# A Fourier filter with an FFN behind it: the first transform of seven batches in three products of rounded parts

## The chip, the cores and the metric

The kernel runs on one core of a Trainium2 chip. Five engines work side by side, each through its own queue in order: TensorE (PE) multiplies matrices into PSUM, VectorE (DVE), ScalarE (ACT) and GpSimd (POOL) work elementwise, and SyncE (SP) issues the transfers. The metric is device time in microseconds of one launch; lower is better.

## The reference

A batch of 8 sequences of 3008 tokens with 256 channels goes through a real Fourier transform along the sequence, a complex 256 x 256 product, a soft threshold and the inverse transform. The result goes through a gated FFN.

```python
X = np.fft.rfft(x, axis=1)
Yr = Xr @ w_r - Xi @ w_i + b_r
Yi = Xr @ w_i + Xi @ w_r + b_i
Yr = np.sign(Yr) * np.maximum(np.abs(Yr) - lam, 0.0)
Yi = np.sign(Yi) * np.maximum(np.abs(Yi) - lam, 0.0)
y = np.fft.irfft(Y, n=x.shape[1], axis=1)
...
g = x @ w_gate
silu = g * (1.0 / (1.0 + np.exp(-g)))
val = x @ w_val
return (silu * val @ w_out).astype(np.float32)
```

## The kernel before

The length 3008 is 47 x 64, and the transform is done as two small transforms in a row. `stage_a` (L290) does the one of length 47: a chunk of x, 96 x 512, is multiplied by the constant `wa` (96 x 96) in one fp32 product (L295), ScalarE copies the result out of PSUM (L298), and it goes to device memory as d1 (L299). There are 16 chunks to a batch, 128 in all. `stage_b` (L304) reads a pair of rows of d1 and does the transform of length 64 (L311); ScalarE copies it out (L315), GpSimd adds real and imaginary parts (L316), and DVE makes two rounded parts of it, `f_hi` (L318) and `f_lo` (L319).

A number in two parts, hi (rounded to the fp32r type) and lo (what the rounding left, also fp32r), is multiplied in three products, hi by hi, lo by hi and hi by lo, as the table `PASSES` says. `stage_mix` (L322) does the complex product so (L329, L337), with a bias added on DVE (L331) between its two halves. Then comes the soft threshold: ScalarE copies t out of PSUM (L349), DVE clamps it to y (L350), GpSimd subtracts (L351), ScalarE rounds to `y_hi` (L354), DVE takes `y_lo` (L355). `stage_bi` (L357) is the first inverse transform, again in three products (L365, L368), copied out by ScalarE (L370) and stored as d2. `stage_ai` (L384) does the second one in fp32 (L388), with a copy out for each half of the channels (L395). Meanwhile `load_seven` (L236) unpacks and splits the FFN's weights on DVE (L223 to L232), GpSimd (L233 to L247, L255) and ScalarE (L254), 18 times.

The order of this part is written as a table of slots. A slot is one pair of rows p of one batch b: stage_b at slot s, stage_mix at s + 1, stage_bi at s + 2, with 12 slots to a batch and 8 batches. The chunks of batches 1 to 7 are put beside them: the first 40 at 2.7 to a slot, the other 72 spread evenly up to slot 84. A chunk is loaded at slot s and goes through stage_a at s + 1. The chunks of batch 0 run before the slots begin. Weight steps begin at slot 14, one block each 4.3 slots. This is the order in which the code is written; the framework's scheduler then gives each engine its own queue order by a timeline of its own. An engine starts its instructions in that order, and one that waits holds all behind it.

The chunks land in five places of 512 columns in a tile named `scratch`. The pools that matter are `early`, `late`, `k1p` and `z`; the class `sb` says by a tag which pool a tile is from.

Behind the transform, `gated_ffn` multiplies the result by the FFN's weights (L516 is the line of all its products), in an order written by hand.

Of the kernel before, what the change touches and what calls it, by code (L numbers as in the profile page):

```python
# [10 lines left out]
F32R = mybir.dt.float32r  # L11
I32 = mybir.dt.int32
AF = mybir.ActivationFunctionType
ALU = mybir.AluOpType
# [3 lines left out]
P = 128  # L18
B = 8
# [8 lines left out]
NCH = NM // CM  # L28
# [4 lines left out]
T = 512  # L33
# [8 lines left out]
LEAD = 1  # L42
X_FAST, X_RATE, X_END = 40, 2.7, 84
# [70 lines left out]
def f32(ap):  # L114
    return ap.bitcast(F32)


PASSES = ((0, 0), (0, 1), (1, 0))


@with_exitstack
def spectral_ffn(ctx: ExitStack, tc: tile.TileContext, xp, w_r, w_i, cb, wup_raw, wdn_raw, ca, cf, ci, co, out):
    nc = tc.nc
    const = ctx.enter_context(tc.tile_pool(name="const", bufs=1))
    dram = ctx.enter_context(tc.tile_pool(name="dram", bufs=2, space=DRAM))
    wdn = [const.tile([P, NQ, 7, P], F32R, name=f"wdn_{p}") for p in ("hi", "lo")]
    ring = ctx.enter_context(tc.tile_pool(name="ring", bufs=RING, reuse_waits="tile"))
    xt_d = [dram.tile([P, 2, SEQ], F32, name=f"xt_d{b}", bufs=1) for b in range(B)]
    d2 = {B - 1: dram.tile([NK, P, C], F32, name="d2_last", bufs=1)}
    wup_d = [dram.tile([P, 2, 7 * P], F32, name=f"wup_d{u}", bufs=1) for u in range(2 * NQ)]  # L130


    front = ctx.enter_context(tc.tile_pool(name="front", bufs=1))
    ps_ = ctx.enter_context(tc.tile_pool(name="ps", bufs=1, space=PSUM))

    with ExitStack() as tail:
        last = tail.enter_context(tc.tile_pool(name="last", bufs=2, side="right"))
        with ExitStack() as one:
            finish = transform(one, tc, front, last, ps_, xp, w_r, w_i, cb, wup_raw, wdn_raw, ca, cf, ci, co, wdn, wup_d, xt_d, d2)
        finish()  # L140
        ffn = gated_ffn(ctx, tc, front, ring, ps_, co, wdn, wup_d, xt_d, d2[B - 1], out)
        next(ffn)
    next(ffn, None)


def transform(ctx, tc, front, last, ps_, xp, w_r, w_i, cb, wup_raw, wdn_raw, ca, cf, ci, co, wdn, wup_d, xt_d, d2):
    nc = tc.nc
    v = nc.vector

    pools = [ctx.enter_context(tc.tile_pool(name=n, bufs=b)) for n, b in (("early", 2), ("late", 2), ("k1p", 1), ("z", 2))]  # L150
    k1p = pools[2]

    class sb:
        at = dict(a_in=0, a=0, f=0, f_hi=0, f_lo=0, raw=1, t=1, y=1, y_hi=1, y_lo=1, both=1, z=3)

        def tile(shape, dtype, name, tag, **kw):
            return pools[sb.at[tag]].tile(shape, dtype, name=name, tag=tag, **kw)
# [9 lines left out]


    wa = k1p.tile([96, 96], F32, name="wa")
    wi = [k1p.tile([P, 2, P], F32R, name=f"wi_{p}") for p in ("hi", "lo")]  # L170
    wmix = [[k1p.tile([P, 2, C], F32R, name=f"wm{i}_{p}") for p in ("hi", "lo")] for i in range(3)]
    bias = []
# [2 lines left out]

    def load_wa():
        nc.sync.dma_start(wa, ca)

    def load_wf(i):
        sl = slice(i, i + 6)  # L180
        nc.sync.dma_start(wf[:, sl, :], cf[:, sl, :])
# [82 lines left out]
    def paced(fn):  # L264
        with tc.issue_after(gates[-1].ins) if gates else ExitStack():
            return fn()

    def load_x(b, ch):
        t = take()
        nc.sync.dma_start(t, xp[b, ch])  # L270
        return t
# [3 lines left out]
    def load_first():  # L275
# [11 lines left out]
            res += [t[:, i * T : (i + 1) * T] for i in range(n)]  # L287
        return res

    def stage_a(b, ch, xt):  # L290
        if ch == 0:
            d1[b] = dram.tile([NK, P, C], F32, name="d1", tag="d1")
        tag = "absz"[ch % 4] if b == 0 else "a"
        ps = ps_.tile([P, T], F32, name="ps_a", tag="ps_" + tag)
        nc.tensor.matmul(ps[:96], lhsT=wa, rhs=xt, start=True, stop=True)  # L295
        tag = "azt"[ch % 3] if b == 0 else "a"
        a = sb.tile([96, T], F32, name="a", tag=tag)
        nc.scalar.copy(a, ps[:96])  # L298
        store = nc.sync.dma_start(d1[b].rearrange("k (q m) c -> (k q) (m c)", m=NM)[:, ch * T : (ch + 1) * T], a)  # L299
        if b == 0 and ch == NCH - 1:  # L300
            gates.append(store)
# [100 lines left out]
    def at(slot, fn):  # L402
        slots.setdefault(int(slot), []).append(fn)

    xs, zs, fs, ys, box = {}, {}, {}, {}, {}
# [5 lines left out]
    for b in range(B):  # L411
        base = NP * b
        for p in range(NP):
            s = base + p
# [2 lines left out]
            at(s + 2, lambda b=b, p=p: stage_bi(b, p, ys.pop((b, p))))  # L417
    for k in range((B - 1) * NCH):
        b, ch = k // NCH + 1, k % NCH
        s = k / X_RATE if k < X_FAST else X_FAST / X_RATE + (k - X_FAST) * (X_END - LEAD - X_FAST / X_RATE) / ((B - 1) * NCH - X_FAST)  # L420
        at(s, lambda b=b, ch=ch: xs.__setitem__((b, ch), paced(lambda: load_x(b, ch))))
        at(s + LEAD, lambda b=b, ch=ch: stage_a(b, ch, xs.pop((b, ch))))
    for k in range((B - 1) * NU):
        b, u = divmod(k, NU)
        s = NP + Z_FIRST + k / Z_RATE if k < Z_LATE else Z_AT + (k - Z_LATE) * Z_STEP
# [11 lines left out]
    for _ in range(WARM):  # L437
        nc.tensor.matmul(mixed[0][:, :C], lhsT=warm[:, :P], rhs=warm[:, C:], start=True, stop=True)
    load_wa()
    first = load_first()  # L440
    gates.append(first_load[-1])
    paced(lambda: load_wf(0))
    for ch in range(NCH):
        stage_a(0, ch, first[ch])
# [374 lines left out]
```

## Time and profile before

| | us |
|---|---|
| median of 3 runs | 2769.14 |
| lowest and highest | 2768.75, 2771.31 |
| the profiled execution's own time | 2764.52 |
| its span in the profile | 2762.6 |
| last product of the inverse transform, start | 674.20 |
| first product of the FFN, start | 676.61 |

In the profile, a group of instructions is a line of the code, an engine and an operation, with the tiles it writes and reads; "busy" is the time in which at least one of them ran, the mean is that of one instruction, and "idle before" is how long the engine stood still ahead of them, and for whom. A wait is written as who waited, for whom, how long in total, how often, and the longest. An fp32 product is recorded as two matmuls, an fp32r product as one.

### The profile page before, as it was taken

How to read it: one execution, taken by the hardware profiler on the slowest of the kernel's cores; microseconds unless marked ns; L12 is line 12 of the kernel's file. 1: busy time of each engine (PE TensorE's matmuls, PEld its weight loads, DVE VectorE, ACT ScalarE, POOL GpSimd, SP SyncE). 2: the span in 40 equal slices, each digit the busy share in tenths (PEclk: the TensorE clock that was granted, in tenths of full speed). 3: DMA queues.
4: the chain of work that ended last, by engine and by line, in shares of the span. 5: the costliest groups of instructions: out<-in, count | busy, mean ns of one | idle time of the engine just before them, and what ended most of it. 6: DMA issues, size and time to landing. Idle time of an engine off the chain costs nothing. (4 is left out here: it accounts for less than half of the span.)

```text
span 2762.6 us, 39633 instructions
## 1 busy us (share of the span) xinstructions
PE 2684.7 (97%) x13173; PEld 2200.4 (80%) x13173; DVE 2157.9 (78%) x2916; ACT 1718.8 (62%) x3280; POOL 2096.8 (76%) x1574
## 2 busy tenths in 40 slices
PE   8999999889999999999999999999999999999998
PEld 5777787787888888888888888888888888888898
DVE  3777677774788888888788878888788888888887
ACT  4666666666656665666665665666666666666665
POOL 1555556554888888888888898889888898888885
PEclk9999999999999999999999999999999999999999
DMA  8889987765344444444444444454444444444453
GB/s 248 263 269 296 305 295 245 235 208 181 134 162 158 155 151 146 167 157 152 139 160 169 152 153 144 159 169 140 148 161 155 162 141 144 152 163 149 148 179 108
DMA packets 180124, 491.88 MB, mean 178 GB/s; under 512 B 17264, under 2 KB 89584, under 8 KB 179824
## 3 DMA queue, kind: packets, MB, share of 16 engines
q1 hardware_dynamic: 179920, 489.35, 53.5%
q8 instruction: 105, 1.72, 0.3%
q14 instruction: 99, 0.81, 0.1%
HBM read 378.65 MB, written 110.62 MB: 177 GB/s over the span
## 5 line engine op out<-in xcount | busy, mean ns | idle before, releaser
L516 PE MATMUL bank<-x_parts,wup 128*128 128x512 f32 (+1 forms) x6048 | 1530.6, 387 | 1.2 <-POOL x_parts L511 0.7
L516 PEld LDWEIGHTS bank<-x_parts,wup 128*128 128x128 f32 x6048 | 1122.6, 188 | 239.2 <-DVE bank L645 22.3
L536 POOL TENSOR_TENSOR h_parts<-more,h_parts 128x512 fp32r<-128x512 f32 (+1 forms) x573 | 846.3, 1492 | 97.8 <-ACT h_parts L532 84.2
L536 POOL TENSOR_TENSOR h_parts<-hidden,h_parts 128x512 fp32r<-128x512 f32 (+1 forms) x432 | 602.9, 1408 | 210.1 <-ACT h_parts L532 167.3
L516 PE MATMUL bank<-h_parts,wdn_hi 128*128 128x512 f32 (+1 forms) x2016 | 627.2, 389 | 2.1 <-POOL h_parts L536 0.9
L532 ACT CAST h_parts<-hidden 128x512 fp32r<-128x512 f32 (+1 forms) x432 | 265.1, 614 | 451.8 <-DVE hidden L618 451.8
L516 PEld LDWEIGHTS bank<-h_parts,wdn_hi 128*128 128x128 f32 x2016 | 378.1, 188 | 97.3 <-POOL h_parts L536 26.3
L618 DVE TENSOR_TENSOR hidden<-hidden,bank 128x512 f32<-128x512 f32 (+1 forms) x576 | 375.9, 674 | 77.8 <-PE bank L516 69.2
L557 DVE TENSOR_TENSOR sums<-sums,bank 128x512 f32<-128x512 f32 (+1 forms) x360 | 241.8, 672 | 228.5 <-PE bank L516 228.4
L532 ACT CAST h_parts<-more 128x512 fp32r<-128x512 f32 (+1 forms) x576 | 351.7, 611 | 103.6 <-DVE more L527 94.9
L516 PE MATMUL bank<-h_parts,wdn_lo 128*128 128x512 f32 (+1 forms) x1008 | 388.9, 386 | 4.2 <-DVE sums L557 4.2
L527 DVE TENSOR_TENSOR more<-hidden 128x512 f32<-128x512 f32 (+1 forms) x288 | 341.0, 1222 | 0.0
L616 ACT ACTIVATE hidden<-bank 128x512 f32<-128x512 f32 (+1 forms) x432 | 252.1, 583 | 85.5 <-PE bank L516 79.4
L527 DVE TENSOR_TENSOR more<-hidden,more 128x512 f32<-128x512 f32 (+1 forms) x288 | 284.5, 988 | 0.0
L351 POOL TENSOR_TENSOR t<-t,y 128x512 f32<-128x512 f32 x96 | 132.5, 1380 | 132.6 <-DVE y L350 132.6
L623 ACT COPY bank<-bank 128x512 f32<-128x512 f32 (+1 forms) x288 | 161.6, 561 | 109.4 <-DVE hidden L618 104.0
L645 DVE TENSOR_TENSOR bank<-hidden,bank 128x512 f32<-128x512 f32 (+1 forms) x288 | 196.3, 681 | 37.2 <-PE bank L516 27.4
L516 PEld LDWEIGHTS bank<-h_parts,wdn_lo 128*128 128x128 f32 x1008 | 189.5, 188 | 41.2 <-issue 4.5
L511 POOL TENSOR_TENSOR x_parts<-xf,x_parts 128x512 fp32r<-128x512 f32 (+1 forms) x168 | 210.5, 1272 | 11.5 <-PE bank L516 7.1
L316 POOL TENSOR_TENSOR f<-f 128x256 f32<-128x256 f32 x96 | 84.0, 875 | 149.7 <-ACT f L315 146.7
L631 ACT COPY hidden<-bank 128x512 f32<-128x512 f32 (+1 forms) x288 | 167.3, 581 | 2.6
L349 ACT COPY t<-mixb 64x256 f32<-64x256 f32 x384 | 140.6, 366 | 25.9 <-PE mixb L337 16.2
(94 smaller groups left out, 3280.4 us busy)
## 6 DMA issues: line engine op xcount, KB each, us to landing
wup<-wup_d SPq DMA_DIRECT2D x288, 896.0 KB, 4.6
d<-a SPq DMA_DIRECT2D x128, 192.0 KB, 4.3
a_in<-d SPq DMA_DIRECT2D x96, 256.0 KB, 4.4
out<-o SPq DMA_DIRECT2D x88, 256.0 KB, 6.1
scratch<-xp SPq DMA_DIRECT2D x116, 192.0 KB, 4.8
d<-z SPq DMA_DIRECT2D x84, 256.0 KB, 3.9
z_in<-d SPq DMA_DIRECT2D x56, 384.0 KB, 5.2
xt_d<-xt SPq DMA_DIRECT2D x56, 376.0 KB, 4.4
```

Source lines behind the costliest of these rows:

```text
L349: nc.scalar.copy(t[64 * half : 64 * half + 64, k * C : (k + 1) * C], mixb[64 * k : 64 * k + 64, half * C : (half + 1) * C])
L511: g.tensor_tensor(part[:, 1, :h], src, f32(part[:, 0, :h]), op=ALU.subtract)
L516: nc.tensor.matmul(o, lhsT=weights[w], rhs=parts[x], start=start and i == 0, stop=stop and i == 2, skip_group_check=True)
L527: v.tensor_tensor(at(o, h), at(a, h), at(b, h), op=ALU.subtract)
L532: act.copy(pair[i][:, 0, :h], at(i, h))
L536: eng.tensor_tensor(pair[i][:, 1, :h], at(i, h), f32(pair[i][:, 0, :h]), op=ALU.subtract)
L557: v.tensor_tensor(o, o, spare[:, :h], op=ALU.add)
L616: act.activation(at(i, h), src, AF.Silu)
L618: v.tensor_tensor(at(i, h), at(i, h), src, op=ALU.mult)
L623: act.copy(b3[:, :h], b1[:, :h])
L631: act.copy(m5, b2[:, :h])
L645: v.tensor_tensor(b2[:, :h], m5, b3[:, :h], op=ALU.add)
```

## The change

The chunks of batches 1 to 7, 112 of the 128, are no longer multiplied in one fp32 product. A new function `split_x` rounds a chunk to `x_hi` on ScalarE and takes what is left, `x_lo`, on GpSimd. `wa` is split once, in `load_wa`, into `wa_hi` (ScalarE) and `wa_lo` (DVE). `stage_a` then makes three products that add up in the same PSUM bank. Batch 0 stays in fp32. Each of the two new tiles has two buffers in the pool `late`. In the table of slots the split stands where stage_a stood, one slot behind the load, and stage_a half a slot later; the loads of the last 72 chunks are drawn in by half a slot so that the last chunk ends where it did.

```diff
+    wa_parts = [k1p.tile([96, 96], F32R, name=f"wa_{p}") for p in ("hi", "lo")]
...
     def load_wa():
         nc.sync.dma_start(wa, ca)
+        nc.scalar.copy(wa_parts[0], wa)
+        v.tensor_tensor(wa_parts[1], wa, f32(wa_parts[0]), op=ALU.subtract)
...
+    def split_x(x):
+        hi = sb.tile([P, T], F32R, name="x_hi", tag="x_hi", bufs=2)[:96]
+        lo = sb.tile([P, T], F32R, name="x_lo", tag="x_lo", bufs=2)[:96]
+        nc.scalar.copy(hi, x)
+        nc.gpsimd.tensor_tensor(lo, x, f32(hi), op=ALU.subtract)
+        return hi, lo
+
     def stage_a(b, ch, xt):
...
-        nc.tensor.matmul(ps[:96], lhsT=wa, rhs=xt, start=True, stop=True)
+        if b == 0:
+            nc.tensor.matmul(ps[:96], lhsT=wa, rhs=xt, start=True, stop=True)
+        else:
+            for n, (w, x) in enumerate(PASSES):
+                nc.tensor.matmul(ps[:96], lhsT=wa_parts[w], rhs=xt[x], start=n == 0, stop=n == 2)
...
-        s = k / X_RATE if k < X_FAST else X_FAST / X_RATE + (k - X_FAST) * (X_END - LEAD - X_FAST / X_RATE) / ((B - 1) * NCH - X_FAST)
+        s = k / X_RATE if k < X_FAST else X_FAST / X_RATE + (k - X_FAST) * (X_END - LEAD - 0.5 - X_FAST / X_RATE) / ((B - 1) * NCH - X_FAST)
         at(s, lambda b=b, ch=ch: xs.__setitem__((b, ch), paced(lambda: load_x(b, ch))))
-        at(s + LEAD, lambda b=b, ch=ch: stage_a(b, ch, xs.pop((b, ch))))
+        at(s + LEAD, lambda b=b, ch=ch: xs.__setitem__((b, ch), split_x(xs.pop((b, ch)))))
+        at(s + LEAD + 0.5, lambda b=b, ch=ch: stage_a(b, ch, xs.pop((b, ch))))
```

The scheduler makes new queue orders of it. The lines of the changed kernel are some 14 higher behind the new function (L351 becomes L365, L316 becomes L330, L354 becomes L368). The first place is GpSimd's queue at the first block of weights (lines 233 to 255 before, 236 to 258 of the change; t is the threshold's subtraction, f the sum of parts). Before:

```order
L233 TENSOR_TENSOR scratch<-scratch 128x512
L351 TENSOR_TENSOR t<-t,y 128x512
L244 TENSOR_TENSOR scratch<-scratch 128x128
L246 TENSOR_TENSOR scratch<-scratch 128x128
L316 TENSOR_TENSOR f<-f 128x256
L245 TENSOR_TENSOR scratch<-scratch 128x128
L247 TENSOR_TENSOR scratch<-scratch 128x128
L255 TENSOR_TENSOR both<-scratch,both 128x896
L351 TENSOR_TENSOR t<-t,y 128x512
```

Of the change, from the same instruction on, GpSimd's queue reads:

```order
L236 TENSOR_TENSOR scratch<-scratch 128x512
L365 TENSOR_TENSOR t<-t,y 128x512
L297 TENSOR_TENSOR x_lo<-scratch,x_hi 96x512
L247 TENSOR_TENSOR scratch<-scratch 128x128
L249 TENSOR_TENSOR scratch<-scratch 128x128
L330 TENSOR_TENSOR f<-f 128x256
L297 TENSOR_TENSOR x_lo<-scratch,x_hi 96x512
L248 TENSOR_TENSOR scratch<-scratch 128x128
L330 TENSOR_TENSOR f<-f 128x256
L365 TENSOR_TENSOR t<-t,y 128x512
L250 TENSOR_TENSOR scratch<-scratch 128x128
L297 TENSOR_TENSOR x_lo<-scratch,x_hi 96x512
```

An x_lo now stands between the pieces of the weight block and ahead of the next f or t; the block's last subtraction (L258) comes three more instructions later.

The second place is ScalarE's queue around the cast of the same block (`both`). Before:

```order
L349 COPY t<-mixb_121 64x256 x4
L254 CAST both<-scratch 128x896
L298 COPY a<-ps_a 96x512
L315 COPY f<-ps_b 128x4x2x64
L370 COPY z<-ps_z 128x512
L349 COPY t<-mixb_120 64x256 x4
L354 CAST y_hi<-t 128x512
```

Of the change, ScalarE's queue at that cast reads:

```order
L368 CAST y_hi<-t 128x512
L312 COPY a<-ps_a 96x512
L296 CAST x_hi<-scratch 96x512
L257 CAST both<-scratch 128x896
L329 COPY f<-ps_b 128x4x2x64
L409 COPY xt<-ps_x_1989 128x376
L409 COPY xt<-ps_x_1995 128x376
L368 CAST y_hi<-t 128x512
```

Each copy of a chunk's result is now followed by the cast of a chunk two further on, which stands ahead of the next f or y_hi.

The third place is TensorE's queue behind the six products of line 329 (343 of the change) of an early slot. Before:

```order
L329 MATMUL ps_s<-wm_hi,f_lo 128x256
L329 MATMUL ps_s<-wm_lo,f_hi 128x256
L295 MATMUL ps_a<-scratch,wa 96x512
L311 MATMUL ps_b<-wf,a_in 128x128 x4
L365 MATMUL ps_z<-y_hi,wi_hi 128x256
```

Of the change, TensorE's queue there reads:

```order
L343 MATMUL ps_s<-wm_hi,f_lo 128x256
L343 MATMUL ps_s<-wm_lo,f_hi 128x256
L309 MATMUL ps_a<-x_hi,wa_hi 96x512
L309 MATMUL ps_a<-x_lo,wa_hi 96x512
L309 MATMUL ps_a<-x_hi,wa_lo 96x512
L379 MATMUL ps_z<-y_lo,wi_hi 128x256
```

One product in fp32 has become three in fp32r, with rounded products ahead of and behind them at this place.

More of the change, by code (lines that the diff above doesn't have):

```diff
@@ L153, in transform @@
     class sb:
-        at = dict(a_in=0, a=0, f=0, f_hi=0, f_lo=0, raw=1, t=1, y=1, y_hi=1, y_lo=1, both=1, z=3)
+        at = dict(a_in=0, a=0, f=0, f_hi=0, f_lo=0, raw=1, t=1, y=1, y_hi=1, y_lo=1, both=1, z=3, x_hi=1, x_lo=1)
         def tile(shape, dtype, name, tag, **kw):
```

## The prediction

> **What bounds the kernel now.** I read the page's first part, then the busy time by stretch, the waits of the longest stretch, its groups of instructions, and single rows of TensorE where prices were needed.
>
> ```profile
> span 2762.6 us, 39633 instructions
> PE 2684.7 (97%) x13173; PEld 2200.4 (80%) x13173; DVE 2157.9 (78%) x2916; ACT 1718.8 (62%) x3280; POOL 2096.8 (76%) x1574
> ```
>
> The share of 97% says TensorE bound, but it is an average over two stages. The next view cuts the span: start-up, the transform's quick first part, its middle, its tail, and the FFN. Columns are window, length, then busy us (count) of PE, PEld, DVE, ACT and POOL, then clock, DMA share and GB/s.
>
> ```profile
> 50.00:100.00 50.00, 49.71 (x313) 40.02 (x313) 30.85 (x49) 38.44 (x84) 19.72 (x19) 1.00 0.76 235
> 100.00:575.00 475.00, 434.12 (x2858) 359.33 (x2857) 352.41 (x479) 308.34 (x672) 264.99 (x239) 0.98 0.84 271
> 575.00:676.00 101.00, 91.32 (x682) 84.55 (x681) 63.39 (x89) 65.51 (x149) 47.24 (x42) 0.95 0.64 205
> 676.00:2762.00 2086.00, 2072.89 (x9201) 1695.50 (x9201) 1700.69 (x2283) 1287.26 (x2343) 1759.89 (x1265) 1.00 0.45 153
> ```
>
> From 676 us on TensorE works 2072.89 of 2086 us, and the change does not touch that stage: whatever the transform gains or loses is passed to the end one to one. The change acts in 35 to 575 us. How fast that part runs is seen by counting: one DVE instruction of line 331 per pair of rows (a slot), two records of line 295 per chunk of x, one ACT copy of line 395 per half of an output unit. The next three fences are windows of lines 331, 295 and 395 alone, in that order.
>
> ```profile
> 50.00:100.00 50.00, 6.90 (x10) 1.00 0.76 235
> 100.00:575.00 475.00, 46.85 (x68) 0.98 0.84 271
> ```
>
> ```profile
> 50.00:100.00 50.00, 15.57 (x30) 4.19 (x30) 1.00 0.76 235
> 100.00:575.00 475.00, 97.94 (x186) 26.22 (x186) 0.98 0.84 271
> ```
>
> ```profile
> 100.00:575.00 475.00, 38.01 (x82) 0.98 0.84 271
> ```
>
> 10 slots in 50 us are 5.0 us each, with 15 chunks; 68 slots in 475 us are 7.0 us each, with 93 chunks and 82 output copies. To see what TensorE truly needs, I take starts, not durations, since its records overlap:
>
> ```profile
> 51.13 1.02 PE L295 MATMUL ps_a<-scratch,wa 96*96 96x512 f32 x2
> 51.99 1.05 PE L311 MATMUL ps_b<-wf,a_in 128*128 128x128 f32 x8
> ...
> 57.41 0.48 PE L368 MATMUL ps_z<-y_hi,wi_hi 128*128 128x512 f32 x1
> 57.73 0.39 PE L368 MATMUL ps_z<-y_lo,wi_hi 128*128 128x512 f32 x1
> 57.96 0.39 PE L368 MATMUL ps_z<-y_hi,wi_lo 128*128 128x512 f32 x1
> 58.19 1.02 PE L295 MATMUL ps_a<-scratch,wa 96*96 96x512 f32 x2
> ...
> 643.51 1.03 PE L388 MATMUL ps_x<-wo,z_in 96*128 96x94 f32 x8
> 644.32 0.48 PE L368 MATMUL ps_z<-y_hi,wi_hi 128*128 128x512 f32 x1
> ```
>
> A chunk takes 51.99 - 51.13 = 0.86 us, half an output unit 0.81 us. In 50 to 100 us TensorE is full, so a slot without its 1.5 chunks costs 49.71/10 - 1.5 x 0.86 = 3.7 us. The middle then needs 68 x 3.7 + 93 x 0.86 + 82 x 0.81 = 398 us of its 475: TensorE really stands idle for some 77 us (16%). Who it waits for, and who those wait for, is in the waits of 100 to 575 us (us in total, times, longest):
>
> ```profile
> POOL t L351 <- DVE y L350: 85.4, 31, 6.7
> POOL f L316 <- ACT f L315: 72.9, 23, 6.5
> DVE y_lo L355 <- ACT y_hi L354: 72.8, 37, 5.2
> ACT y_hi L354 <- POOL t L351: 45.8, 42, 2.4
> ACT f L315 <- DVE f_lo L319: 44.2, 33, 3.5
> ...
> DVE f_hi L318 <- PE mixb L337: 20.1, 19, 2.5
> ...
> PE mixb L337 <- DVE mixb L331: 15.7, 21, 1.6
> ...
> PE ps_z L368 <- DVE y_lo L355: 7.7, 7, 2.9
> ```
>
> The middle is a ring with no single bound. The soft threshold goes DVE y, GpSimd t, ScalarE y_hi, DVE y_lo; DVE stands 72.8 us at y_lo, and ScalarE 45.8 us for GpSimd's t behind it. DVE waits only 20.1 us for TensorE. TensorE's longest named wait is the bias add on DVE. So in the middle GpSimd, ScalarE and DVE end more of the waits than TensorE does.
>
> **The change part by part.** The sum is made for the profiled execution of 2764.52 us (span 2762.6 and 1.9 around it); the median of the runs shown, 2769.14, lies 4.6 us higher, and I add the same change to it.
>
> TensorE, 112 chunks. Before: 0.86 us. After: three products of the kind of line 368, whose starts are 57.41, 57.73 and 57.96, with the next work at 58.19: 0.78 us behind a full fp32 product, 0.23 us apart otherwise, so 0.69 at best. The saving is 0.08 to 0.17 us; I take 0.15, since the scheduler puts most new triples behind the rounded products of lines 329 and 337. 112 x 0.15 = 17 us of TensorE's time (9 to 19). All of it counts where TensorE is full (15 chunks, 2 us). Of the other 97, 15 us, I count a quarter, since TensorE has 16% spare there: **-6 us** in all; the ends are 0 and -19.
>
> [...]
>
> ScalarE and GpSimd. Their nearest rows, and DVE's, in the groups of 100 to 575 us (busy us, mean ns of one, idle before it):
>
> ```profile
> L351 POOL TENSOR_TENSOR t<-t,y 128x512 f32<-128x512 f32 x68 | 95.4, 1403 | 85.4 <-DVE y L350 85.4
> L319 DVE TENSOR_TENSOR f_lo<-f,f_hi 128x768 fp32r<-128x768 f32 x69 | 78.8, 1142 | 1.2
> L355 DVE TENSOR_TENSOR y_lo<-t,y_hi 128x512 fp32r<-128x512 f32 x68 | 59.9, 881 | 72.8 <-ACT y_hi L354 72.8
> L318 DVE CAST f_hi<-f 128x768 fp32r<-128x768 f32 x70 | 59.0, 843 | 21.7 <-PE mixb L337 20.1 <-POOL f L316 1.6
> L354 ACT CAST y_hi<-t 128x512 fp32r<-128x512 f32 x69 | 42.8, 620 | 46.4 <-POOL t L351 45.8
> L350 DVE TENSOR_SCALAR y<-t 128x512 f32<-128x512 f32 x68 | 42.4, 623 | 2.3 <-ACT t L349 2.3
> ```
>
> The new x_lo is a subtraction of 512 columns, as line 351: 1.40 us; 112 of them are 157 us, and the 93 of the middle 130 us, which takes GpSimd from 265 to 395 of 475 us (83%). The new x_hi is a cast like line 354: 0.62 us, 93 x 0.62 = 58 us, ScalarE from 308 to 366 (77%).
>
> DVE gets no work but loses speed beside GpSimd. The ranges of its lines from 40 to 660 us (min/median/max ns) show it:
>
> ```profile
> L318 DVE CAST f_hi<-f x95: 542/560/1860, 42.5 to 659.7; 128x768 fp32r<-128x768 f32 x95
> L319 DVE TENSOR_TENSOR f_lo<-f,f_hi x95: 940/957/2836, 39.2 to 654.6; 128x768 fp32r<-128x768 f32 x95
> L350 DVE TENSOR_SCALAR y<-t x93: 406/419/2333, 47.4 to 656.1; 128x512 f32<-128x512 f32 x93
> L355 DVE TENSOR_TENSOR y_lo<-t,y_hi x93: 673/691/2581, 50.7 to 659.1; 128x512 fp32r<-128x512 f32 x93
> L331 DVE TENSOR_TENSOR mixb<-ps_s,bias x94: 680/690/699, 43.0 to 655.5; 128x512 f32<-128x512 f32 x94
> ```
>
> Line 331, with an operand in PSUM, never varies; the four that read SBUF alone are stretched up to threefold. Mean less minimum: 0.30 + 0.20 + 0.22 + 0.21 = 0.93 us a slot, 63 us in 68 slots, with GpSimd busy 265 us: 0.24 us of DVE time for each us of GpSimd. A new x_lo thus costs DVE 1.40 x 0.24 = 0.34 us, 33 us for the 97 chunks outside the full stretch. DVE is busy 352 of 475 us (74%) and in the ring; half of it counts: **+17 us** (0 to +33).
>
> [...]
>
> Waiting in queues. The rows on GpSimd and ScalarE start in a fixed order, shown above this prediction: x_lo stands ahead of t or f, and x_hi ahead of y_hi. GpSimd is on x_lo for 130 of 475 us (27%); a t that comes then waits 0.7 us on average: 0.27 x 0.7 = 0.19 us, for 68 t and 69 f 26 us, and I count a third, as 37 of 68 y_lo wait and f seldom holds DVE: **+8 us** (0 to +26). An x_hi that is late itself holds all behind it. ScalarE: 58/475 = 12% times 0.3 us, for seven ScalarE rows in each of 68 slots 17 us, a third: **+5 us** (0 to +17).
>
> Nothing for the rest: the split of wa at the start is one small instruction each on ScalarE and DVE, while ScalarE waits for the first product anyway; if uncovered, under 1 us by line 354's 0.62. The loads keep size and lead; their places come free by x_lo instead of the product, which SyncE's queue already waits for:
>
> ```profile
> SPq L270 <- PE ps_a L295: 29.5, 25, 3.4
> ```
>
> If x_lo comes late, the load behind it and the stores queued behind that load are late with it; I leave this in the range.
>
> Sum: -6 + 17 + 8 + 5 = **+24 us**: 2764.5 + 24 = 2788.5 for a profiled run, 2769.1 + 24 = **2793** for the median.
>
> **The rivals.** First, faster: x_lo fits into time that GpSimd wastes. It waited 31 times for y, 2.8 us on average, and 23 times for f, 3.2 us; an x_lo of 1.40 us that lands in such a wait delays nobody, and ScalarE's order splits two chunks ahead, so TensorE has its parts in time. It decides from whether most of the 93 fall into these 54 waits. Then only TensorE's saving is left, 9 to 19 us: 2750 to 2760, say 2752. Against it: 93 are more than 54, and the weights' bursts on GpSimd leave no wait at all.
>
> Second, no change: saving and delays cancel, 2769. Third, GpSimd becomes the bound in the slots with weight work. All of the stretch (33), all t and f waits (26) and ScalarE's (17) count, 76, with no saving: 2845. For it: lines 351 and 354 are in the ring now. Against: GpSimd still has 17% spare. Fourth, the change does not do what it says: three products at 0.78 us and a switch each way save nothing. That gives +30 by the other terms, 2799, inside the forecast.
>
> **How the numbers follow.** What a measurement can tell from no change is about 0.2%, 5.5 us. Forecast, slower by 8 to 66 us, with the fourth rival in it: 0.55. GpSimd as bound, above that: 0.10. Same: 0.13. Faster: 0.22. So slower 0.65. The range goes from 2752, where the faster case is half in, to 2835, which leaves out the third rival: about 2 in 10 are out. The forecast's own range is 2777 to 2835.
>
> **What would show it.** In the changed profile: starts of a triple 0.69 to 0.78 us apart from the next work; x_lo near 1.4 us; means of lines 318, 319, 350 and 355 up by 15 to 30% while line 331 stays at 0.69; the wait of y_hi for t above 45.8 us; the FFN's length unchanged at 2086 us. It is wrong if DVE's waits for y_hi stay as they are, if the slots of the middle come below 7.0 us, or if the FFN's start moves for another reason.

## The result and the profile after

| | before | after |
|---|---|---|
| median, us | 2768.94 | 2837.36 |
| lowest and highest, us | 2764.84, 2771.31 | 2834.87, 2841.01 |
| the profiled execution's own time, us | 2764.52 | 2835.54 |
| first product of the FFN, start, us | 676.61 | 747.71 |

The change makes the kernel slower by 68 us: the ratio is 1.0247, with a 95% interval of 1.0227 to 1.0266. The sign is that of the forecast, the size is nearly three times its +24. The lines of the changed kernel: x_hi 296, x_lo 297, the three products 309, f 329 and 330, f_hi 332, f_lo 333, the bias 345, t 363, y 364, the subtraction of t 365, y_hi 368, y_lo 369, the first inverse transform 382.

The first part of the page of the changed kernel:

```profile
span 2833.4 us, 40171 instructions
PE 2696.8 (95%) x13285; PEld 2243.1 (79%) x13285; DVE 2313.4 (82%) x2917; ACT 1776.1 (63%) x3393; POOL 2277.6 (80%) x1686
```

DVE was given one small instruction, and its busy time rose by 155 us, from 2157.9 to 2313.4. GpSimd was given 112 subtractions and rose by 181. The busy time by stretch, with the columns as in the prediction, says where; the last row is the FFN:

```profile
50.00:100.00 50.00, 42.86 (x281) 36.34 (x280) 46.26 (x45) 39.29 (x85) 41.89 (x30) 1.00 0.62 193
100.00:575.00 475.00, 398.56 (x2604) 354.99 (x2603) 419.12 (x419) 314.42 (x676) 358.25 (x291) 0.92 0.76 245
575.00:676.00 101.00, 82.86 (x581) 74.52 (x580) 88.09 (x97) 63.69 (x138) 68.73 (x58) 0.95 0.60 190
747.00:2833.00 2086.00, 2072.66 (x9201) 1695.64 (x9201) 1700.87 (x2283) 1287.16 (x2344) 1759.98 (x1265) 1.00 0.45 153
```

The FFN takes 2086 us as before, so the whole loss is in the transform. In the middle DVE now works 419 of 475 us (88%, before 74%), with 60 fewer instructions than before (419 against 479). TensorE fell from 434 to 399 us, its granted clock from 0.98 to 0.92. The windows of the bias add alone (line 345, one to a slot) count the slots:

```profile
50.00:100.00 50.00, 6.17 (x9) 1.00 0.62 193
100.00:575.00 475.00, 41.27 (x60) 0.92 0.76 245
```

60 slots in 475 us are 7.9 us each, where 68 had been 7.0. The waits from 100 to 575 us (us in total, times, longest) show who is late now:

```profile
ACT f L329 <- DVE f_lo L333: 53.4, 23, 4.2
...
PE mixb L351 <- DVE mixb L345: 41.3, 31, 2.9
POOL t L365 <- DVE y L364: 39.7, 28, 3.7
ACT y_hi L368 <- POOL t L365: 32.0, 28, 3.2
POOL x_lo L297 <- ACT x_hi L296: 28.1, 19, 4.1
...
POOL f L330 <- ACT f L329: 20.5, 12, 3.1
PE ps_z L382 <- DVE y_lo L369: 20.2, 16, 3.8
```

TensorE's wait for the bias add rose from 15.7 to 41.3 us, its wait for y_lo from 7.7 to 20.2. GpSimd's waits for y and f were used up (85.4 to 39.7, 72.9 to 20.5), yet y_hi waits less for GpSimd's t than before (45.8 to 32.0). The engine that is late is DVE. The groups of the same stretch (busy us, mean ns of one, idle before it and for whom) show why:

```profile
L297 POOL TENSOR_TENSOR x_lo<-scratch,x_hi 96x512 fp32r<-96x512 f32 x84 | 128.4, 1528 | 28.1 <-ACT x_hi L296 28.1
...
L369 DVE TENSOR_TENSOR y_lo<-t,y_hi 128x512 fp32r<-128x512 f32 x60 | 86.3, 1440 | 16.0 <-ACT y_hi L368 15.9
L333 DVE TENSOR_TENSOR f_lo<-f,f_hi 128x768 fp32r<-128x768 f32 x60 | 82.5, 1375 | 0.9
L332 DVE CAST f_hi<-f 128x768 fp32r<-128x768 f32 x60 | 73.7, 1229 | 25.5 <-PE mixb L351 19.0 <-POOL f L330 3.0 <-POOL scratch L250 2.3
L364 DVE TENSOR_SCALAR y<-t 128x512 f32<-128x512 f32 x61 | 46.8, 767 | 3.4 <-ACT t L363 3.4
L345 DVE TENSOR_TENSOR mixb<-ps_s,bias 128x512 f32<-128x512 f32 x60 | 41.3, 688 | 1.8 <-PE ps_s L343 1.7
```

The four DVE operations of the ring that work in SBUF alone have grown: y_lo from 881 to 1440 ns, f_hi from 843 to 1229, f_lo from 1142 to 1375, y from 623 to 767. The bias add, with an operand in PSUM, takes 688 as before. The unpacking of the weights on DVE (lines 226 to 235), eight instructions a step that also work in SBUF alone, has grown too, from 5.5 to 7.7 us a step. DVE's wait for y_hi fell from 72.8 to 15.9 us: its slack was eaten by its own longer instructions.

One stretch of the timeline shows how a single instruction grows. Columns are start, length, engine, line. GpSimd:

```profile
421.13 1.28 POOL L297 TENSOR_TENSOR x_lo<-scratch,x_hi 96x512 fp32r<-96x512 f32 x1
...
424.12 2.09 POOL L258 TENSOR_TENSOR both<-scratch,both 128x896 fp32r<-128x896 f32 x1
426.19 1.18 POOL L330 TENSOR_TENSOR f<-f 128x256 f32<-128x256 f32 x1
427.33 1.58 POOL L297 TENSOR_TENSOR x_lo<-scratch,x_hi 96x512 fp32r<-96x512 f32 x1
```

And DVE in the same 8 us:

```profile
421.37 1.64 DVE L369 TENSOR_TENSOR y_lo<-t,y_hi 128x512 fp32r<-128x512 f32 x1
424.84 1.93 DVE L369 TENSOR_TENSOR y_lo<-t,y_hi 128x512 fp32r<-128x512 f32 x1 [1.83 <-ACT y_hi L368]
426.69 1.09 DVE L332 CAST f_hi<-f 128x768 fp32r<-128x768 f32 x1
427.82 1.90 DVE L333 TENSOR_TENSOR f_lo<-f,f_hi 128x768 fp32r<-128x768 f32 x1
```

Each of the four ends as if it had begun only when the GpSimd instruction beside it ended. The first y_lo: x_lo ends at 422.41, and 0.67 us (the shortest y_lo) later is 423.08; it ended at 423.01. The f_lo: x_lo ends at 428.91, plus 0.94 (the shortest f_lo) is 429.85; it ended at 429.72. The f_hi and the second y_lo end as close, 0.13 and 0.11 us ahead of that reckoning. So at these places DVE does not share with GpSimd: the four rows are 3.74 us longer than the shortest of their lines, of 4.18 us that they stood beside the GpSimd instruction.

The timelines of both engines from 100 to 575 us show the same for all rows of these four lines. Before the change, 102 of 275 rows began while a GpSimd instruction ran (four that began within 0.05 us of its start are left out, as is one after the change), and each ended within 0.16 us of that instruction's end plus the shortest time of the line. After it, 144 of the 239 rows that the timeline shows singly began so, and 130 of them ended so. The other 14 stood still through two or more GpSimd instructions in a row, which no row did before. One of them is a y_lo that began beside a sum f and ended only behind the next f, the fifth GpSimd instruction in its way (GpSimd's row, then DVE's):

```profile
314.28 0.72 POOL L330 TENSOR_TENSOR f<-f 128x256 f32<-128x256 f32 x1
...
310.78 4.78 DVE L369 TENSOR_TENSOR y_lo<-t,y_hi 128x512 fp32r<-128x512 f32 x1
```

That f ends at 315.00, plus 0.67 is 315.67; the y_lo ended at 315.56. Why GpSimd passes DVE by several times in a row at some places and once at others is not shown.

### The profile page after: what moved, and what is told of

The parts are those of the page before. It is cut to its first block, busy times and chain, and to the rows that moved or that the text cites. A ratio compares the mean times of both kernels' runs of the same rounds, so it can differ in the third digit from the quotient of the medians.

```text
span 2833.4 us, 40171 instructions
## 1 busy us (share of the span) xinstructions
PE 2696.8 (95%) x13285; PEld 2243.1 (79%) x13285; DVE 2313.4 (82%) x2917; ACT 1776.1 (63%) x3393; POOL 2277.6 (80%) x1686
## 5 line engine op out<-in xcount | busy, mean ns | idle before, releaser
L297 POOL TENSOR_TENSOR x_lo<-scratch,x_hi 96x512 fp32r<-96x512 f32 x112 | 172.9, 1545 | 67.3 <-ACT x_hi L296 67.1
L365 POOL TENSOR_TENSOR t<-t,y 128x512 f32<-128x512 f32 x96 | 138.2, 1440 | 77.5 <-DVE y L364 69.2
L351 PE MATMUL mixb<-wm_hi,f_hi 128*128 128x256 f32 x384 | 121.3, 316 | 56.5 <-DVE mixb L345 56.0
```

Of the source, the lines that this page charges most:

```text
L297: nc.gpsimd.tensor_tensor(lo, x, f32(hi), op=ALU.subtract)
```

## The experiments

Medians come from fresh runs beside the kernel before, whose median was 2768.2 to 2769.1 us in them; each ratio is to it, with its 95% interval. Diffs are against the changed kernel where nothing else is said. The theories: **contention** (x_lo costs what it takes from DVE), **queue** (x_lo holds up t and f behind it on GpSimd), **ScalarE** (the casts hold up ScalarE's queue), **order** (the new table of slots costs by itself).

### Without x_lo, and with x_lo elsewhere

**e1_no_lo.** x_lo is not made; the second product (the expectation calls it the third) reads x_hi again, so the lower part of x is left out and the upper one counted twice there. ScalarE's casts, the three products and the slots stay.

```diff
-        lo = sb.tile([P, T], F32R, name="x_lo", tag="x_lo", bufs=2)[:96]
-        nc.gpsimd.tensor_tensor(lo, x, f32(hi), op=ALU.subtract)
-        return hi, lo
+        return hi, hi
```

> The changed kernel without x_lo: the third product reads x_hi again, so TensorE and ScalarE do the same work and GpSimd none of the new. Contention theory (GpSimd's new subtraction stretches DVE): about 2769 - 6 + 5 = 2768 us, 2755 to 2775, with the means of DVE's lines back near 0.81, 1.12, 0.58 and 0.85 us. GpSimd-queue theory (x_lo delays t and f) gives the same time, so this run does not tell the two apart. ScalarE theory (x_hi ahead of f and y_hi is the cost): still 2820 or more. Schedule theory (the new order is the cost): still 2820 or more.

2748.63 us, ratio 0.9931 (0.9914 to 0.9947): below the range that any theory gave. Without x_lo the change is 20 us faster than the kernel before, with it 68 slower: x_lo costs 89 us, and ScalarE's casts and the slots cannot be the cause. DVE's busy time on the page falls from 2313.4 to 2171.2. Its groups from 100 to 575 us:

```profile
L331 DVE TENSOR_TENSOR f_lo<-f,f_hi 128x768 fp32r<-128x768 f32 x72 | 84.3, 1170 | 0.9
L367 DVE TENSOR_TENSOR y_lo<-t,y_hi 128x512 fp32r<-128x512 f32 x71 | 70.9, 999 | 43.3 <-ACT y_hi L366 43.3
L330 DVE CAST f_hi<-f 128x768 fp32r<-128x768 f32 x72 | 62.3, 866 | 39.8 <-PE mixb L349 39.7
...
L362 DVE TENSOR_SCALAR y<-t 128x512 f32<-128x512 f32 x71 | 36.8, 518 | 2.4 <-ACT t L361 2.4
```

The means are back near those of before, and DVE waits for y_hi again (43 us). 142 us of DVE's time over 112 chunks are 1.27 us for each x_lo. Contention and queue both allow the 89 us; the next runs part them.

**e6_lo_dve.** x_lo is made on DVE instead of GpSimd.

```diff
-        nc.gpsimd.tensor_tensor(lo, x, f32(hi), op=ALU.subtract)
+        v.tensor_tensor(lo, x, f32(hi), op=ALU.subtract)
```

> The changed kernel with x_lo on DVE instead of GpSimd: 112 subtractions of 0.69 us are 77 us of work on DVE, GpSimd has its old load. Against the run without x_lo (2749 us). If half of DVE's added time ends in the total, as the prediction counted: 2749 + 39 = 2788 us (2775 to 2800), some 50 us faster than the changed kernel, because GpSimd's x_lo took about 140 us from DVE and DVE's own takes 77. If all of it ends there: 2826. Queue theory (what costs is x_lo ahead of t and f on GpSimd, not DVE's time): 2760 or less.

2788.5 us, 1.0069 (1.0043 to 1.0094), 49 faster than the change. That is the 2788 of contention; the queue theory had 2760 or less. The new work in the groups of 0 to 800 us:

```profile
L297 DVE TENSOR_TENSOR x_lo<-scratch,x_hi 96x512 fp32r<-96x512 f32 x112 | 108.4, 970 | 29.1 <-ACT x_hi L296 28.7 <-PE ps_a L309 0.3
```

Here DVE does all 108 us of x_lo itself, and its busy time on the page is 2250.2, **63 us less** than when GpSimd does them. Given to GpSimd, an x_lo takes more from DVE (1.27 us) than if DVE makes it (0.97).

**e2_fill.** x_lo is filled with zeros by three GpSimd memsets that together last about as long, so the lower part of x is zero; GpSimd writes SBUF and reads nothing there.

```diff
-        nc.gpsimd.tensor_tensor(lo, x, f32(hi), op=ALU.subtract)
+        for _ in range(3):
+            nc.gpsimd.memset(f32(lo), 0.0)
```

> The changed kernel with x_lo filled with zeros by three GpSimd instructions of about 0.5 us each that read nothing, in place of the subtraction of 1.55 us (the output lacks x_lo). GpSimd is as long in the way of t and f as in the changed kernel, but reads no operand. Contention theory, if it is the reading that stretches DVE: 2760 to 2790 us, with DVE's means near those of before. GpSimd-queue theory: 2820 to 2845 us, as in the changed kernel. If writing alone holds DVE too, DVE's means stay up and the time stays above 2815, and the two theories are not told apart.

2803.53 us, 1.0124 (1.0109 to 1.0139): between the two, so it doesn't decide. Its groups from 100 to 575 us say why:

```profile
L298 POOL MEMSET x_lo<- 96x512 f32 x264 | 145.0, 560 | 25.8 <-PE ps_a L310 22.1
L334 DVE TENSOR_TENSOR f_lo<-f,f_hi 128x768 fp32r<-128x768 f32 x63 | 80.7, 1281 | 0.8
L333 DVE CAST f_hi<-f 128x768 fp32r<-128x768 f32 x64 | 76.8, 1200 | 41.7 <-PE mixb L352 38.6 <-POOL x_lo L298 1.9 <-PE ps_b L326 0.6
L370 DVE TENSOR_TENSOR y_lo<-t,y_hi 128x512 fp32r<-128x512 f32 x63 | 61.3, 972 | 17.3 <-ACT y_hi L369 16.9
L365 DVE TENSOR_SCALAR y<-t 128x512 f32<-128x512 f32 x62 | 45.2, 730 | 5.8 <-ACT t L364 5.7
```

Against e1_no_lo the operations with one input have grown (f_hi 866 to 1200 ns, y 518 to 730), those with two hardly (f_lo 1170 to 1281, y_lo 999 to 972). The fill was no neutral stand-in: it keeps about half of the contention (70 of 142 us of DVE's busy time).

**e10_hi_t_dve and e9_swap.** Both move the subtraction of t from GpSimd to DVE, so that y_hi no longer waits for anything behind x_lo on GpSimd. e9_swap is the change with that; e10_hi_t_dve has no x_lo and only two products, with x at the precision of its upper part.

```diff
-        nc.gpsimd.tensor_tensor(t, t, y, op=ALU.subtract)
+        v.tensor_tensor(t, t, y, op=ALU.subtract)
```

e10_hi_t_dve has, besides:

```diff
+        return hi, hi
...
-            for n, (w, x) in enumerate(PASSES):
-                nc.tensor.matmul(ps[:96], lhsT=wa_parts[w], rhs=xt[x], start=n == 0, stop=n == 2)
+            for n in range(2):
+                nc.tensor.matmul(ps[:96], lhsT=wa_parts[n], rhs=xt[0], start=n == 0, stop=n == 1)
```

> Two products of x_hi without x_lo (x at the precision of its upper part), and t - y on DVE. If the two gains add (-19 and -25): 2725 us (2715 to 2735), faster than both kernels and than either edit alone. If both shorten the same waits: 2740 to 2745.

> The changed kernel with the threshold's subtraction t - y on DVE: GpSimd has x_lo in t's place, about its old load, and no t behind x_lo. By the account so far (run without x_lo 2749; t on DVE -25; half of what x_lo takes from DVE, 120 to 140 us, +60 to 70; no t to wait behind x_lo): 2784 to 2794 us, 45 to 55 faster than the changed kernel. Queue theory alone (x_lo costs only by standing ahead of t and f): 2730 or less. If DVE at its limit is the bound: 2810 or more.

e10_hi_t_dve: 2724.12 us, 0.9843 (0.9819 to 0.9867), as expected if the two gains add, and faster than both kernels, though with x in fewer digits. e9_swap: 2813.82 us, 1.0162 (1.0144 to 1.0181), some 20 above the best guess and where DVE at its limit was expected (2810 or more): DVE is busy 434.52 of 475 us in its middle. The queue theory had 2730 or less. Freeing t from the queue gained 24 us, no more than the same edit gains without any x_lo (e7_t_dve, below). So t behind x_lo in the queue was not the price. Between the two, DVE's busy time is 2195.0 and 2318.4. They also differ by one product, which by e8_two (below) is worth nothing.

**e14_lo_none and e13_lo_alone.** t and the sum of f are both moved to DVE; of the ring nothing is left on GpSimd. e13_lo_alone keeps x_lo there, beside the weights; e14_lo_none leaves it out as e1_no_lo does.

```diff
-        nc.gpsimd.tensor_tensor(f[:, 2 * C :], f[:, :C], f[:, C : 2 * C], op=ALU.add)
+        v.tensor_tensor(f[:, 2 * C :], f[:, :C], f[:, C : 2 * C], op=ALU.add)
...
-        nc.gpsimd.tensor_tensor(t, t, y, op=ALU.subtract)
+        v.tensor_tensor(t, t, y, op=ALU.subtract)
```

> The same without x_lo (the third product reads x_hi again), t - y and the sum of f on DVE: by the runs with t alone and with t and f on DVE, which differ by 3 us, 2724 + 3 = 2727 us (2715 to 2740) by either theory.

> The changed kernel with both t - y and the sum of f on DVE: on GpSimd x_lo has only the weights beside it, and nothing of the chain from f to y_lo stands behind it. Contention theory: 80 to 100 us above the run of the same kernel without x_lo, about 2815 us (2800 to 2835), with DVE over 90% busy. Queue theory (x_lo ahead of f and t): at most 40 us above that run, 2770 or less.

2723.86 us, 0.9834 (0.9817 to 0.9852), and 2789.8 us, 1.0068 (1.0051 to 1.0085): x_lo costs 66 us where no step of the ring can queue behind it. That is less than the 80 to 100 of contention and more than the 40 that the queue theory allowed. The middle of e14_lo_none, in the columns of the windows above:

```profile
100.00:575.00 475.00, 451.22 (x3242) 411.64 (x3241) 417.46 (x677) 381.05 (x828) 126.33 (x108) 0.98 0.89 288
```

And that of e13_lo_alone:

```profile
100.00:575.00 475.00, 416.64 (x2830) 372.83 (x2829) 445.40 (x587) 341.43 (x734) 255.86 (x185) 0.95 0.82 263
```

With x_lo DVE does 90 instructions less in the middle and is busy 28 us longer. GpSimd is at 256 of 475 us and far from full. Here no step of the ring stands behind x_lo, and TensorE waits 2.4 us in all for x_lo itself. The loads of x wait for it as well, since it holds their places: SyncE 68.3 us here and 71.7 in the change, from 100 to 575 us. But the transfers still come in time: TensorE waits for them 2.9 us here and 2.3 in the change, against 5.0 before. What is left is the contention.

The five pairs with and without x_lo, worked out from the medians and from DVE's busy time on the pages:

| without | with | time, us | DVE busy, us | us of time per us of DVE |
|---|---|---|---|---|
| e1_no_lo | the change | +88.7 | +142.2 | 0.62 |
| e1_no_lo | e6_lo_dve | +39.9 | +79.0 | 0.51 |
| e1_no_lo | e2_fill | +54.9 | +70.4 | 0.78 |
| e10_hi_t_dve | e9_swap | +89.7 | +123.4 | 0.73 |
| e14_lo_none | e13_lo_alone | +65.9 | +102.2 | 0.64 |

The time follows what DVE loses, at 0.5 to 0.8. The change and e13_lo_alone have the same 0.62 and 0.64, one with t and f behind x_lo in GpSimd's queue, one without: a price of the queue itself does not show. The 23 us by which x_lo costs less in e13_lo_alone go with 40 us less that DVE loses. The spread of the column leaves room for some 10 to 20 us of a queue's price.

### The other parts of the change

**e3_split_only.** x_hi and x_lo are made and not read; x is multiplied in fp32.

```diff
-        return hi, lo
+        return x
...
-        if b == 0:
-            nc.tensor.matmul(ps[:96], lhsT=wa, rhs=xt, start=True, stop=True)
-        else:
-            for n, (w, x) in enumerate(PASSES):
-                nc.tensor.matmul(ps[:96], lhsT=wa_parts[w], rhs=xt[x], start=n == 0, stop=n == 2)
+        nc.tensor.matmul(ps[:96], lhsT=wa, rhs=xt, start=True, stop=True)
```

> The changed kernel with the split made but not used: stage_a multiplies x by wa in one fp32 product as before. All the costs on ScalarE and GpSimd, none of TensorE's saving. If TensorE's saving is worth the 6 us of the prediction: 2843 us (2838 to 2850). If it is worth all of 17 us: 2854. If the three products are what costs, as with TensorE in the way: 2790 or less.

2844.27 us, 1.0272 (1.0257 to 1.0287), as expected. The three products are worth 7 us in the change; in this figure is also that x's place is held here until the fp32 product has read it, and in the change only until the split.

**e4_order_only.** The kernel before with the new table of slots alone.

```diff
-... (X_END - LEAD - X_FAST / X_RATE) ...
+... (X_END - LEAD - 0.5 - X_FAST / X_RATE) ...
-        at(s + LEAD, lambda b=b, ch=ch: stage_a(b, ch, xs.pop((b, ch))))
+        at(s + LEAD + 0.5, lambda b=b, ch=ch: stage_a(b, ch, xs.pop((b, ch))))
```

> The kernel before with only the table of slots of the change: stage_a half a slot later and the loads drawn in by half a slot; no split, one fp32 product. Contention theory: no difference, 2769 us (2763 to 2775). Schedule theory (the new order is a part of the cost): 2785 or more.

2776.1 us, 1.0025 (1.0013 to 1.0036): half a slot more between load and product costs 7 us here, where x keeps its place until the product. The prediction had put the table of slots at nothing.

**e12_hi_only.** Only x_hi is made, and not read; x is multiplied in fp32 as in e3_split_only.

```diff
-        lo = sb.tile([P, T], F32R, name="x_lo", tag="x_lo", bufs=2)[:96]
-        nc.gpsimd.tensor_tensor(lo, x, f32(hi), op=ALU.subtract)
-        return hi, lo
+        return x
```

> The changed kernel with only the cast x_hi on ScalarE, which nothing reads; stage_a multiplies x in one fp32 product. Against the run with the same table of slots and no split (2776): if ScalarE's cast costs the 5 us of the prediction, 2781 us (2771 to 2793). If it is ScalarE that costs: 2800 or more.

2777.43 us, 1.0034 (1.0018 to 1.005), inside the range: ScalarE's casts cost 1 us over e4_order_only, which the intervals do not tell from nothing.

**e5_pe_only.** No split at all; the three products read a rounded tile of weights instead of x, so x is left out.

```diff
-... rhs=xt[x], start=n == 0, stop=n == 2)
+... rhs=wmix[0][0][:96].rearrange("p a c -> p (a c)"), start=n == 0, stop=n == 2)
...
-        at(s + LEAD, lambda b=b, ch=ch: xs.__setitem__((b, ch), split_x(xs.pop((b, ch)))))
```

> Three fp32r products in stage_a without any split: they read a rounded tile of weights in place of x's parts (the output lacks x there), the order is the half slot later of the change. Only TensorE's saving is left: 2763 us by a quarter of 17 us (2757 to 2768), 2752 if all of it counts, 2769 if none. Above 2790 the three products or the new order themselves would be the cost.

2762.19 us, 0.9982 (0.9971 to 0.9993), as expected: 14 us below e4_order_only. Not all of it need be TensorE's saving, since nothing reads x here and its places come free at once: SyncE's loads wait for no product, where in e4_order_only they waited 16.8 us for stage_a's (100 to 575 us).

**e8_two.** As e1_no_lo, with two products of x_hi instead of three (x at the precision of its upper part).

> The changed kernel without x_lo and without its product: two products, x_hi by both parts of wa (x is taken at the precision of its upper part). Contention theory: a little under the run with three products and no x_lo, 2749 - 112 x 0.23 x 1/4 = 2743 us (2735 to 2750), faster than both kernels. If TensorE's time counted in full: 2723.

2749.78 us, 0.9927 (0.9907 to 0.9948), at the upper end of the range: 1 us from e1_no_lo. A third product less, 112 times 0.23 us, brings nothing.

### The same engine pair in the kernel before

**e7_t_dve** is the kernel before with t's subtraction on DVE, **e11_t_f_dve** with t's and f's sum there (the diffs of e9_swap and e13_lo_alone).

> The kernel before with the threshold's subtraction t - y moved from GpSimd to DVE. By overlap in the trace of before, t on GpSimd stretches DVE by about 52 x 0.68 = 35 us, and on DVE it takes 96 x 0.69 = 66 us: DVE's load rises by about 31 us, half of that is +15, and the ring y, t, y_hi, y_lo loses a hop and 0.7 us a turn, which may give as much back. Contention theory: 2755 to 2785, best 2769, with DVE's remaining lines nearer to their minima. If GpSimd's reading costs DVE nothing, +66 on DVE: 2800 or more.

> The kernel before with both t - y and the sum of f on DVE, so that GpSimd has only the weights in the transform. DVE gets 96 x 0.42 = 40 us more than with t alone and loses the stretch by the sum, 45 us of overlap x 0.4 = 18 us: +22, half of it +11, less the hop from GpSimd to DVE ahead of f_hi. 2735 to 2760 us, best 2750. If GpSimd's reading is dear beside DVE wherever it stands: 2735 or less.

e7_t_dve: 2743.53 us, 0.9904 (0.9886 to 0.9922), faster by 25 us than before and than the best guess, and below the expected range. e11_t_f_dve: 2746.34 us, 0.9921 (0.9904 to 0.9937), inside its range. Both compute what the kernel before does, and they are the fastest that leave x in full precision; the intervals do not tell them apart. e7_t_dve's groups from 100 to 575 us:

```profile
L351 DVE TENSOR_TENSOR t<-t,y 128x512 f32<-128x512 f32 x70 | 60.1, 858 | 1.3
L318 DVE CAST f_hi<-f 128x768 fp32r<-128x768 f32 x71 | 52.6, 741 | 16.6 <-PE mixb L337 10.6 <-POOL f L316 5.6 <-PE ps_s L329 0.3
...
L350 DVE TENSOR_SCALAR y<-t 128x512 f32<-128x512 f32 x71 | 36.2, 510 | 2.6 <-ACT t L349 2.6
```

t takes 858 ns on DVE where GpSimd took 1403, f_hi falls from 843 to 741 and y from 623 to 510. On the page DVE's busy time rises by 39 us (2157.9 to 2197.3), for 84 us of work that it took over.

## Why the prediction was right in sign and wrong in size

The view that mattered was read rightly: the middle is a ring in which TensorE waits, DVE slows beside GpSimd, the bias add does not (689 ns before, 688 after), and the FFN passes on what the transform loses (2086 us again). The sizes, term by term:

| term | predicted, us | the runs |
|---|---|---|
| x_lo: stretch of DVE and GpSimd's queue | +17 and +8 | +89 together (e1_no_lo to the change) |
| everything else | -6 and +5 | -20 (before to e1_no_lo) |
| sum | +24 | +68 |

**The step that failed is the stretch of DVE.** It said "0.24 us of DVE time for each us of GpSimd. A new x_lo thus costs DVE 1.40 x 0.24 = 0.34 us, 33 us for the 97 chunks", of which half counts. An x_lo took 1.53 us and cost DVE 1.27 (142 us over 112); "half counts" was near, at 0.62. The ratio was an average: all of the stretch by all of GpSimd's time, and the price of a further instruction is another. Mean less the minima that the prediction lists, for the same four lines: 0.69 + 0.44 + 0.36 + 0.77 = 2.25 us a slot, 135 us in 60 slots at 358 us of GpSimd; before it was 63 us at 265. The added 93 us of GpSimd brought 72 us of stretch, 0.77 for each us, three times the average. The ratio also left out DVE's unpacking of the weights, whose eight lines read SBUF alone too: by the same reckoning their stretch went from 23 to 53 us. And where the prediction reads "up to threefold", its own row of y goes from 406 to 2333 ns, over fivefold: single rows already said more than the mean.

Why it is three times shows when the overlaps are added up from the timelines of both engines, 100 to 575 us (rows whose lengths, added, come 2 to 3% above GpSimd's busy time):

| | before | after | added |
|---|---|---|---|
| GpSimd's rows, us | 271 | 368 | 97 |
| of it beside the four DVE lines, us | 127 | 223 | 96 |
| stretch of these lines, us | 64 | 136 | 72 |
| stretch for each us beside them | 0.51 | 0.61 | 0.75 |

Before, less than half of GpSimd's time fell on the four lines. The whole of what was added falls on them. By the rows counted in the section on the result, the added stretch has two parts: more rows of DVE were held by one GpSimd instruction (130 against 102, which is 92 us of stretch against 61), and 14 were held by several in a row, 40 us, where none had been. In e1_no_lo, without x_lo, none was held by several.

The timeline of a single stretched instruction would have shown more: a row of DVE that stands still until GpSimd's ends, as here in the kernel before, GpSimd's row and then DVE's:

```profile
122.06 2.39 POOL L255 TENSOR_TENSOR both<-scratch,both 128x896 fp32r<-128x896 f32 x1 [1.06 <-ACT both L254]
...
123.15 1.73 DVE L318 CAST f_hi<-f 128x768 fp32r<-128x768 f32 x1 [0.66 <-PE mixb L337]
```

`both` ends at 124.45, plus 0.54, the shortest f_hi, is 124.99; the f_hi ended at 124.88.

**GpSimd's queue, +8.** Not seen by itself (e13_lo_alone against the change). The sign that was to show it, y_hi's wait for t above 45.8 us, failed: it fell to 32.0.

**ScalarE, +5.** Measured 1, not told from nothing (e4_order_only to e12_hi_only).

**TensorE, -6.** The pairs give 7 us in the change (e3_split_only), 14 without any split (e4_order_only to e5_pe_only) and 29 with x_hi alone (e12_hi_only to e1_no_lo), each with a part that comes from x's places. In the last pair the casts also free x's places in `scratch` early: ScalarE's groups from 100 to 575 us, in e12_hi_only:

```profile
L295 ACT CAST x_hi<-scratch 96x512 fp32r<-96x512 f32 x92 | 57.1, 621 | 30.1 <-DMA scratch<-xp 29.4
```

and in e1_no_lo:

```profile
L295 ACT CAST x_hi<-scratch 96x512 fp32r<-96x512 f32 x92 | 57.3, 622 | 2.3 <-PE ps_a L307 1.8 <-ACT xt L407 0.2
```

The casts wait for loads where the fp32 product holds the place. That alone does not account for the 15 us between the last two pairs: in e5_pe_only the places come free at once too, and yet e1_no_lo, with the casts on top, is 14 us faster than it. The cause of these stays open, and with it how the 20 us divide by which e1_no_lo beats the kernel before. The products themselves were priced rightly, 0.69 us for three (below).

**The table of slots, at nothing.** It costs 7 us where x keeps its place until the product (e4_order_only). In the change the split reads x half a slot earlier, so how much of the 7 us is in it was not measured.

**Late loads, left in the range.** Over the whole execution SyncE's loads waited 102.1 us for x_lo, against the 29.5 us for the product that the prediction shows. It held up little: TensorE waited for transfers no longer than before (2.3 us in the middle, 5.0 before).

**The rivals.** The first, faster: x_lo did move into GpSimd's waits, which shrank by 98 us, and still delayed others, because its price is not GpSimd's time. The third had nearly the right time (2845) by luck, since its engine is the wrong one: GpSimd is not the bound at 358 of 475 us, DVE is nearly so at 419. Against the fourth, that three products save nothing, stand the 7 us of e3_split_only.

**The signs.** Means of the four DVE lines: said 15 to 30% up, measured 20% (f_lo), 23% (y), 46% (f_hi), 63% (y_lo). x_lo: said near 1.4 us, measured 1.53. Of what was to show it wrong, the slots are not below 7.0 but at 7.9, and DVE's waits for y_hi did not stay, they fell from 72.8 to 15.9 us.

## What to carry to other kernels

Elementwise work in SBUF that was moved to GpSimd beside a busy DVE was not free here: an x_lo of 1.53 us on GpSimd took 1.27 us from DVE, 0.8 for each microsecond, where DVE needed only 0.97 us to make it itself. Price such a move by the overlap that the new load will have, from single stretched instructions in the timeline, and never by the average of the load before. Where two engines share a ring, try also the way back: one subtraction taken from GpSimd to DVE made the kernel before 25 us faster.

## What the runs showed of the hardware that was not expected

**GpSimd's memsets slowed DVE's subtractions less than its x_lo did.** The memsets of e2_fill stretched DVE's casts and clamps, with one input each, by 39 and 41%, and its subtractions by 9 and -3%; x_lo stretched the subtractions too (y_lo by 44 and f_lo by 18% over e1_no_lo). Why is not shown.

**TensorE's granted clock was lower in the kernels where it stood idle longer.** The granted clock in the middle is 0.98 before and in e1_no_lo, 0.92 in the change. Over ten of the sixteen kernels (the two, e1_no_lo, e2_fill, e6_lo_dve, e7_t_dve, e9_swap, e10_hi_t_dve, e13_lo_alone and e14_lo_none) it goes with TensorE's idle time there: 0.96 to 0.98 where TensorE stood idle 24 to 53 of the 475 us, 0.92 to 0.95 where it stood idle 58 to 76. The timeline of TensorE in the change, around such a place:

```profile
302.22 0.50 PE L382 MATMUL ps_z<-y_lo,wi_hi 128*128 128x512 f32 x1 [2.29 <-DVE y_lo L369]
302.56 0.40 PE L382 MATMUL ps_z<-y_hi,wi_lo 128*128 128x512 f32 x1
304.24 0.46 PE L351 MATMUL mixb<-wm_hi,f_hi 128*128 128x256 f32 x1 [1.28 <-DVE mixb L345]
304.50 0.42 PE L351 MATMUL mixb<-wm_hi,f_lo 128*128 128x256 f32 x1
304.71 0.42 PE L351 MATMUL mixb<-wm_lo,f_hi 128*128 128x256 f32 x1
...
307.07 0.63 PE L309 MATMUL ps_a<-x_hi,wa_hi 96*96 96x512 f32 x1
...
308.11 0.28 PE L343 MATMUL ps_s<-wm_hi,f_lo 128*128 128x256 f32 x1
308.23 0.28 PE L343 MATMUL ps_s<-wm_lo,f_hi 128*128 128x256 f32 x1
...
315.95 0.39 PE L309 MATMUL ps_a<-x_hi,wa_hi 96*96 96x512 f32 x1
...
316.64 0.40 PE L382 MATMUL ps_z<-y_hi,wi_lo 128*128 128x512 f32 x1
```

At 315.95 three products take 0.69 us to the next start, as predicted. Before 304.24 TensorE had two waits with 0.74 us of work between them; after that products of 256 columns start 0.21 us apart, where at 308 us they take 0.12, and three products take 1.04 us. The windows of this stretch give the granted clock: 1.00 up to 304 us, 0.60 from 304 to 306, 0.50 to 307, 0.59 to 308, and 1.00 after that. So at this place the wait on DVE is paid twice, once while it lasts and once in slow products behind it. Not every wait is: the one ahead of 315.61, for the y_lo that was held through five GpSimd instructions, lasted 2.30 us, and the products behind it ran at 1.00. If the clock's 0.06 had been lost over all of TensorE's work in the middle, 399 x (1 - 0.92/0.98) gives 24 us, an estimate; how much of the 68 us it is was not separated, since in the change, e9_swap and e13_lo_alone, with x_lo on GpSimd, the clock (0.92, 0.93 and 0.95) fell together with DVE's stretch.
